# Two units' k and q transposed by DMA instead of by TensorE, in a retention and token-mixing kernel with a hand-written order

## The chip, the cores and the metric

The kernel runs on one core of one Trainium2 chip (trn2). The metric is the time of one launch on the device in microseconds; for the kernel before, the median of three runs is 164.52 us (164.24 to 164.79). Everything that is read from a profile comes from one further, profiled execution.

## The reference

Two stages, cut to what matters:

```python
# q, k, v: (4, 8, 768, 64) float32 (batch, heads, sequence, head width)
for t in range(S):                                    # per batch and head
    state = gamma * state + outer(k[t], v[t])
    y[t] = (1 / sqrt(D)) * q[t] @ state
x = heads side by side                                # (4, 768, 512)
theta = x @ w_theta
z_r, z_i = x * cos(theta), x * sin(theta)
u = x + w_tok_r @ z_r + w_tok_i @ z_i                 # mixes tokens: (768 x 768) @ (768 x 512), per batch
out = u + max(u @ w_ch, 0)
```

The recurrence is computed in chunks: inside a chunk of tokens as masked attention, from chunk to chunk through the state.

## The kernel before

The attention work is cut into 24 units. Unit n is one batch, 256 tokens (two chunks of 128) and half of the heads, so six units make a batch. The mixing work is cut into 24 tiles of 128 tokens. Units and tiles overlap: the mixing of one batch runs while the attention of the next one is under way.

Nothing schedules this but a table. `ORDER` is a long string of tokens; the kernel walks through it and calls one small function for each token, and each engine executes its instructions in just that order. A token is a step's name, its unit or tile, and sometimes the engine: `ck.13.a` is the cast of k of unit 13 on ScalarE (ACT), `.v` is VectorE (DVE), `.p` is GpSimd (POOL), `.s` the SyncE (SP) queue. Each engine and queue works its own steps off in order, and waits where data or a buffer is missing; tile pools with a fixed number of buffers decide when a buffer comes free.

The steps of unit n that matter here, with their lines:

- `Lk`, `Lq`, `Lv` (L156): loads of k, q and v of the unit, 256 KB each.
- `ck`, `cq`/`cqs`, `cv` (L136/L138, L304, L310): casts to bf16. k and q of the unit go into one tile kqb (five buffers), v into vb. `cqs` and `cv` multiply by a decay factor on the way.
- Transposing kqb into kqT, in one of three ways. `Tk` and `Tq` (L318) are eight 128x128 TensorE transposes into PSUM and `E` copies them out. `Tk6`, `Tq6` and `E6` (L337) do the same in 64x64 tiles, of which several fit into TensorE's array at once: 32 transposes and two copies. `Dk` (L367) is one DMA transpose, issued by the SP queue, with nothing on TensorE:

```python
    def Dk(n):
        kqT = work.tile([P, 2, 2, 2, P], BF, name="kqT", bufs=4)
        nc.sync.dma_start_transpose(
            out=kqT.rearrange("p w a j t -> p (w a j) t"),
            in_=st["kqb", n].rearrange("p w d -> p (w d)"))
        st["kqT", n] = kqT
```

- `A` (L380): scores from kqT. `m` (L389): mask, on VectorE. `ST` (L408): the unit's part of the state, from kqb and vb. `S0`, `S1` (L426, L430): the state's sums, on VectorE. `SB` (L136/L138): the state as bf16. `I` (L446) and `Y` (L458): output from the state, and from the scores, in the PSUM banks R0 and R1, each of which one unit holds at a time. `I` of a unit writes the banks that the unit before it used, so it waits for that one's `S0` and `S1`.
- `XA`, `XB` (L476, L136/L138): the output out of PSUM, as xT of a chunk. `Tx`, `Tx6`, `Dx` (L490, L337, L504): xT back into token order, by TensorE or by DMA.

And of the mixing:

- `Hh` (L511) is x @ w_theta of a chunk in a PSUM accumulator, `CN` (L518) the sine and cosine passes of ScalarE over it, `z` (L525) the product with x. `M` (L559) are the token-mixing matmuls of a tile, `u` (L566) adds x, `Tu`, `Tu6`, `Du` (L571, L337, L590) transpose u, `O` (L595) multiplies by w_ch, `f` (L601) finishes, `SO` (L606) stores. `Hh`, `M` and `O` share two accumulator banks.

`A`, `Y`, `ST` and all steps named with a 6 work on 64x64 tiles of TensorE's array; all others use the whole array.

Of the kernel before, what the change touches and what calls it, by code (L numbers as in the profile page):

```python
# [50 lines left out]
CN.10.1 Dx.11 Ex.10.v Lk.16.s Lv.17.s Hh.11 SO.2.s CN.10.0 m.12 S1.12 z.10.v cq.13.v M.6.1 M.6.2 M.6.0  # L51
M.6.3 CN.11.0 CN.11.1 M.7.3 SB.12.1.a Lk.17.a ck.13.a M.7.4 M.7.0 M.6.4 Dk.13 M.7.1 z.11.v SO.3.s A.14
Tu6.5 M.6.5 Eu6.5.0.a Eu6.5.1.a M.7.2 I.12 Lv.14.s u.6 cqs.15.v M.7.5 M.9.3 ck.17.a m.14 SO.4.a Lq.17.s
Lq.18.s Lk.21.s ck.16.a M.9.0 M.9.5 M.9.1 M.9.4 Lq.19.a M.9.2 Du.6 cv.13.v u.7 u.9 Y.12 cv.14.p ST.13
Tk6.15 Tq6.15 E6.15.0.v E6.15.1.v A.13 O.5 XB.12.1.a XB.12.0.a M.8.1 S0.13.a S1.13 M.8.4 M.8.3 SB.13.0.a
SB.13.1.p cq.16.p m.13 I.13 ck.18.a Y.13 ST.14 A.15 M.8.0 f.5 cq.17.v Lv.18.a M.8.5 M.8.2 XA.13.0
XA.13.1 S0.14.v SB.14.0.p Lv.16.s Hh.13 S1.14 u.8 M.10.1 cv.15.p cv.17.p SB.14.1.p M.10.0 M.10.4
cqs.18.v M.10.5 CN.13.0 CN.13.1 Hh.12 CN.12.1 I.14 m.15 Y.14 CN.12.0 ST.15 S0.15.v XB.14.1.a SB.15.0.a
M.10.3 cv.16.v Dk.16 Dk.17 Du.7 Dx.13 M.10.2 Dk.18 O.6 SB.15.1.p XB.14.0.v S1.15 I.15 Y.15 ST.16 Tx6.12
SO.5.a cv.18.p f.6 S0.16.v A.16 M.11.4 cq.19.p SB.16.1.p M.11.1 Lq.21.a Ex6.12.0.a Ex6.12.1.a z.12.p  # L60
SB.16.0.a Lk.19.s Lk.20.s XB.15.0.a u.10 z.13.p XB.15.1.a m.16 O.7 Du.10 I.16 Y.16 Tu6.8 ST.17 f.7
Eu6.8.0.v Eu6.8.1.a A.17 Hh.15 CN.15.1 CN.15.0 Dx.14 M.11.2 Tx.15 Lv.22.s SO.7.s M.11.0 M.11.5 S0.17.v
SB.17.0.p M.11.3 XA.16.1 m.17 XA.16.0 Ex.15.v Hh.14 SB.17.1.p z.15.p ck.21.p ck.19.p I.17 u.11 Tu6.11
A.18 Y.17 ST.18 Eu6.11.1.v S0.18.v XA.17.1 XA.17.0 O.10 SO.1.a S1.18 Lv.19.a CN.14.1 CN.14.0 Dx.16
Lq.20.a f.10 Lq.22.a SB.18.0.a Hh.17 Eu6.11.0.a SB.18.1.a I.18 Tk.19 Tq.19 CN.17.1 O.8 CN.17.0 m.18
E.19.a Hh.16 z.14.p Lv.20.s Du.9 f.8 O.11 Y.18 cv.19.p ck.20.a CN.16.1 ST.19 A.19 Tx6.17 CN.16.0 M.12.1
f.11 Ex6.17.0.v Ex6.17.1.v cq.20.p Lk.22.s Dk.20 M.12.0 S0.19.a M.13.3 M.13.2 XB.18.1.a SB.19.1.p
SB.19.0.v M.13.0 z.17.v cqs.21.v XB.18.0.v S1.19 z.16.v m.19 cv.20.v M.12.3 M.12.2 M.13.5 Lv.21.s M.13.1
M.12.4 M.12.5 I.19 M.13.4 Y.19 ST.20 u.12 A.20 Dk.21 XA.19.1 S0.20.v XA.19.0 ck.22.a cq.22.a SB.20.1.p
cv.22.p M.14.3 M.14.5 M.14.1 M.14.4 M.14.2 M.14.0 SB.20.0.p u.13 m.20 S1.20 Hh.19 I.20 Y.20 SO.10.s  # L70
Lq.23.s Lk.23.s cv.21.v u.14 A.21 ST.21 CN.19.0 CN.19.1 S0.21.v M.15.3 M.15.5 S1.21 m.21 XA.20.1 Hh.18
CN.18.1 CN.18.0 Dx.18 Dk.22 ck.23.a M.15.4 M.15.2 SB.21.0.p M.15.1 M.15.0 SB.21.1.v Lv.23.s Du.12 Dx.19
XA.20.0 O.9 f.9 I.21 Y.21 A.22 ST.22 M.16.1 cqs.23.p u.15 m.22 S0.22.v z.18.p z.19.p M.16.5 SB.22.0.p
M.16.4 O.12 M.16.0 SO.8.a M.16.2 M.16.3 SB.22.1.p XB.21.0.a XB.21.1.a SO.11.s Du.14 cv.23.p Dk.23 f.12
Du.13 Dx.20 Dx.21 Hh.21 u.16 I.22 A.23 Y.22 ST.23 CN.21.0 CN.21.1 Hh.20 CN.20.1 S0.23.v XA.22.1 XA.22.0
SB.23.0.a M.17.1 M.17.3 CN.20.0 M.17.0 SB.23.1.p I.23 M.17.2 m.23 Y.23 O.13 M.17.4 z.21.v M.17.5 Mh.0.1
Mh.0.3 XB.23.1.v f.13 Hh.23 u.17 XB.23.0.a SO.13.a CN.23.1 Du.16 Hh.22 z.20.v CN.22.1 Mh.0.2 M.19.3
Dx.23 CN.23.0 Dx.22 Mh.0.0 M.21.1 M.19.1 z.23.p CN.22.0 SO.6.a Du.17 M.18.1 O.16 M.21.2 M.19.2 M.19.0
M.18.3 f.16 SO.9.a M.18.5 z.22.p M.18.2 O.17 M.19.4 M.18.0 Mh.0.4 M.18.4 f.17 u.18 Du.15 SO.12.s O.15
M.19.5 f.15 u.19 SO.16.s M.22.2 M.22.1 O.14 Mh.0.5 uh.0 f.14 M.22.0 M.21.5 M.22.3 M.22.5 Du.19 M.21.4  # L80
SO.17.s M.22.4 Du.18 O.19 M.21.0 M.21.3 M.20.2 Mh.1.2 Mh.1.0 Mh.1.4 u.22 O.18 Mh.1.3 SO.15.a f.19 M.20.0
M.20.1 Tuh.0 u.21 Du.22 Du.21 f.18 M.20.3 Euh.0 M.20.4 Mh.1.1 M.20.5 u.20 O.22 Mh.1.5 uh.1 f.22 Tu.20
SO.14.a SO.19.s Eu.20.a O.21 SO.18.a Tuh.1 Euh.1 f.21 Oa.0 Oa.1 fa.0 fa.1 Oh.0 Oh.1 SO.21.a SO.22.s
SO.20.s fh.0 SOh.0 fh.1 SOh.1 Z.31
""".split()


# [618 lines left out]
```

## Time and profile before

| | |
|---|---|
| median of three runs | 164.52 us (164.24 to 164.79) |
| the profiled execution's own time | 164.61 us |
| its span, first to last instruction | 162.9 us |
| TensorE matmul busy | 154.2 us, 95% of the span |
| VectorE, ScalarE, GpSimd busy | 114.1, 79.6, 72.2 us |
| granted TensorE clock | 1.000 |
| DMA | 34.93 MB, mean 214 GB/s |

How to read it: busy time is what an engine spent in instructions. In a timeline each row is a start in us from the span's start, a duration, the engine, the line in the kernel, the operation, out<-in and a count; neighbouring rows of one kind are merged. Matmuls are pipelined, so the duration of a row overlaps the next one, and the time a step takes from TensorE is the distance from its start to the next start. A DMA's row on SP is the time that its issue took; its landing is told apart.

### The profile page before, as it was taken

The numbers are of one execution on the slowest core, as the hardware profiler recorded it, in microseconds if no ns is written. First come the engines' busy times: TensorE is split into PE (matmuls) and PEld (weight loads), VectorE is DVE, ScalarE is ACT, GpSimd is POOL, SyncE is SP. The second block draws the span as 40 slices with busy tenths as digits, with TensorE's granted clock in tenths as the row PEclk, the third lists the DMA queues.
The fourth block names the chain that finished last, engine by engine and source line by source line (L and its number), as shares of the span: only waits on it lengthen the run. The fifth ranks groups of instructions, "written<-read, shape, count | busy, mean of one in ns | idle before, by whom it ended". The sixth has DMA issues, their size and how long they took to land.

```text
span 162.9 us, 5079 instructions
## 1 busy us (share of the span) xinstructions
PE 154.2 (95%) x2108; PEld 86.0 (53%) x2108; DVE 114.1 (70%) x218; ACT 79.6 (49%) x148; POOL 72.2 (44%) x105
## 2 busy tenths in 40 slices
...
DMA packets 69062, 34.93 MB, mean 214 GB/s; under 512 B 26416, under 2 KB 66096, under 8 KB 69040
## 3 DMA queue, kind: packets, MB, share of 16 engines
...
q10 hardware_dynamic: 10320, 7.47, 16.0%
q0 software_dynamic: 2688, 3.41, 12.1%
q8 instruction: 16, 0.26, 0.7%
q14 instruction: 6, 0.05, 0.1%
...
## 4 chain that ended last, share of the span: by engine, by line
PE 79%; DMA 8%; ACT 5%; SPq 2%; POOL 2%; DVE 1%; issue 1%; POOLq 0%; ACTq 0%
PE y_ps L559 37%; PE o_ps L595 12%; PE th_ps L511 12%; DMA kqf<-in_k_dram 8%; PE r_ps L458 4%; ACT qx L232 3%; PE at_ps L380 3%; PE w_ps L533 2%; PE r_ps L446 2%; SPq L156 2%; PE kq_ps L318 2%; PE y_ps L620 2%; PE r_ps L408 1%; PE x_ps L490 1%; ACT kqb L136 1%
## 5 line engine op out<-in xcount | busy, mean ns | idle before, releaser
L559 PE MATMUL y_ps<-z,wtr 128*128 128x512 bf16 x138 | 52.4, 380 | 0.0
L559 PE MATMUL y_ps<-z,wti 128*128 128x512 bf16 x138 | 52.3, 379 | 0.0
L525 POOL TENSOR_TENSOR z<-cs,x_sb 128x1024 bf16<-128x1024 bf16 x12 | 25.5, 2138 | 17.2 <-ACT cs L518 10.7
L389 DVE TENSOR_TENSOR at<-at_ps,mask 128x1024 bf16<-128x1024 f32 x24 | 29.2, 1216 | 1.0 <-PE at_ps L380 1.0
L310 POOL TENSOR_TENSOR vb<-vf,vsc 128x512 bf16<-128x512 f32 x15 | 15.6, 1042 | 23.3 <-DMA vf<-in_v_dram 19.1
L566 DVE TENSOR_TENSOR u<-y_ps,x_sb 128x512 bf16<-128x512 f32 x23 | 15.8, 688 | 13.2 <-PE y_ps L559 13.1
L511 PE MATMUL th_ps<-wth,xT 128*128 128x512 bf16 x96 | 24.5, 379 | 0.4 <-ACT cs L518 0.4
L601 DVE SCALAR_TENSOR_TENSOR ot<-o_ps,u 128x512 f32<-128x512 f32 x22 | 15.2, 689 | 13.4 <-PE o_ps L595 13.2
L595 PE MATMUL o_ps<-wch,uT 128*128 128x512 bf16 x88 | 22.6, 379 | 0.0
L518 ACT ACTIVATE cs<-th_ps,halfpi 128x512 bf16<-128x512 f32 x24 | 16.3, 685 | 12.5 <-PE th_ps L511 6.9
L518 ACT ACTIVATE cs<-th_ps,zerob 128x512 bf16<-128x512 f32 x24 | 16.5, 686 | 10.6 <-PE th_ps L511 5.1
L559 PEld LDWEIGHTS <-wtr 128*128 128x128 bf16 x138 | 13.5, 98 | 13.2
L559 PEld LDWEIGHTS <-wti 128*128 128x128 bf16 x138 | 13.5, 98 | 12.6 <-issue 0.4
L138 POOL CAST sbd<-s 64x256 bf16<-64x256 f32 (+1 forms) x20 | 8.4, 420 | 21.2 <-DVE s L426 19.5
L136 ACT COPY kqT<-kq_ps 128x1024 bf16<-128x1024 bf16 (+1 forms) x11 | 10.7, 973 | 10.1 <-PE kq_ps L318 9.8
L511 PEld LDWEIGHTS <-xT 128*128 128x128 bf16 x96 | 8.8, 98 | 9.2 <-issue 0.8
L595 PEld LDWEIGHTS <-uT 128*128 128x128 bf16 x88 | 8.1, 98 | 8.3
L279 PE MATMUL zz<-zero 128*128 128x512 bf16 x30 | 10.0, 463 | 1.9 <-DVE zero L191 1.9
L136 ACT CAST kqb<-kqf 128x512 bf16<-128x512 f32 x16 | 9.6, 623 | 4.0 <-DMA kqf<-in_k_dram 4.0
L458 PE MATMUL r_ps<-at,vb 64*64 64x128 bf16 x384 | 10.0, 221 | 1.6 <-DVE at L389 1.6
L380 PE MATMUL at_ps<-kqT 64*64 64x128 bf16 x384 | 10.0, 219 | 0.4 <-DVE kqT L138 0.4
L318 PE MATMUL kq_ps<-ident,kqb 128*128 128x128 bf16 x104 | 9.3, 220 | 0.8 <-POOL kqb L304 0.6
...
## 6 DMA issues: line engine op xcount, KB each, us to landing
...
```

What stands on the lines that cost most here:

```text
L136: nc.scalar.copy(dst, src)
L310: engines[e].tensor_mul(in_blocks(vb), by_token(raw["vf", n]), _bcast_last(K["vsc"][:, i, :, h * HU:(h + 1) * HU], D))
L380: nc.tensor.matmul(at_ps[cols, g, j, a, :], kq_at(n, 0, a, j, c)[rows], kq_at(n, 1, slice(0, 2), j, c)[rows], start=(j == 0 and a == 0), s ...
L389: nc.vector.tensor_mul(at.rearrange("p g j a t -> p (g j) (a t)"), st["at_ps", n].rearrange("p g j a t -> p (g j) (a t)"), _bcast_mid(K["m ...
L458: nc.tensor.matmul(st["R", n + 1][c][g * D:(g + 1) * D, j * P:(j + 1) * P], st["vb", n][rows, lo:lo + D], st["at", n][rows, g, j, a, :], s ...
L511: nc.tensor.matmul(th_ps, st["xT", C][:, j, :], K["wth"][:, j, :], start=(j == 0), stop=(j == 3))
L518: nc.scalar.activation(st["cs", C][:, w, :], st["th_ps", C], AF.Sin, bias=K["zerob" if w else "halfpi"], scale=1.0)
L525: engines[e].tensor_mul(st["z", b][:, c], st["cs", C], _bcast_mid(x_of(C), 2))
L559: nc.tensor.matmul(st["y", t], K["wT"][r][:, s0, t0 * P:(t0 + 1) * P], st["z", b][:, s0, r, :], start=(done == 0 and r == 0), stop=(done = ...
L566: nc.vector.tensor_add(st["u", t], st["y", t], st["x", b][:, t0, :])
L595: nc.tensor.matmul(o_ps, st["uT", t][:, j, :], K["wch"][:, j, :], start=(j == 0), stop=(j == nD - 1))
L601: nc.vector.scalar_tensor_tensor(st["ot", t], st["o", t], 0.0, st["u", t], ALU.max, ALU.add)
```

## The change

Unit 15's `Tk6`, `Tq6` and two `E6`, and unit 19's `Tk`, `Tq` and `E`, are removed; `Dk.15` and `Dk.19` come in. The tokens `Lk.19.s` and `Lk.21.s` change places. Eight other tokens stand elsewhere than before: `Tu.0` (behind A.8), `O.1` (ahead of M.4.0), `ck.13.a` (earlier), `Dx.11` (behind Lk.16), `cqs.15.v` (right behind z.11), `S0.14.v` (ahead of XA.13.1), `ck.19.p` (from behind ck.21 up to behind SB.14.1), `A.18` (from ahead of Y.17 to behind Hh.17); and `I.18` and `Tx6.17` stand in another order to their neighbours than before. No function is changed. Two places of the table, cut:

```diff
-ST.13 Tk6.15 Tq6.15 E6.15.0.v E6.15.1.v A.13 O.5
+ST.13 A.13 O.5
...
-Tu6.11 A.18 Y.17 ST.18 ... O.10 ... Hh.17 Eu6.11.0.a SB.18.1.a I.18 Tk.19 Tq.19 CN.17.1 O.8 ... E.19.a Hh.16 ... O.11 Y.18 ... ST.19 A.19 Tx6.17
+Tu6.11 Y.17 ST.18 ... O.10 ... Hh.17 A.18 Eu6.11.0.a SB.18.1.a Tx6.17 CN.17.1 O.8 I.18 ... Hh.16 ... O.11 Y.18 ... ST.19 A.19
```

On the SP queue around `Dk.15`: the L606 row is the store of tile 3, the vf row the load of v of unit 14, and the rows behind are q of units 17 and 18 and k of unit 21 (before) or 19 (now).

```order
 L606 DMA out_dram<-ot 128x512
 L156 DMA vf<-in_v_dram 128x4x128
+L367 DMA_TRANSPOSE kqT<-kqb 128x8x128
 L156 DMA kqf<-in_q_dram 128x4x128 x2
 L156 DMA kqf<-in_k_dram 128x4x128
```

The transpose of unit 15 stands between a load and three loads that stood right behind one another.

On the SP queue around `Dk.19`: uT is the transpose of u of tile 10, x_sb that of chunk 14, and the vf row the load of v of unit 22.

```order
 L590 DMA_TRANSPOSE uT<-u 128x4x128
 L504 DMA_TRANSPOSE x_sb<-xT 128x4x128
+L367 DMA_TRANSPOSE kqT<-kqb 128x8x128
 L156 DMA vf<-in_v_dram 128x4x128
 L606 DMA out_dram<-ot 128x512
```

The transpose of unit 19 is a third transpose in a row, ahead of a load and a store.

On GpSimd around `ck.19`: the two vb rows in front are cv.15 and cv.17, the sbd rows are SB.14.1 and SB.15.1 (their numbers differ only because tiles are numbered anew), and behind them come cv.18 and cq.19.

```order
 L310 TENSOR_TENSOR vb<-vf,vsc 128x512 x2
-L138 CAST sbd_96<-s_1763 64x4x64
-L138 CAST sbd_98<-s_1990 64x4x64
+L138 CAST sbd_96<-s_1765 64x4x64
+L138 CAST kqb<-kqf 128x512
+L138 CAST sbd_98<-s_1955 64x4x64
 L310 TENSOR_TENSOR vb<-vf,vsc 128x512
 L138 CAST kqb<-kqf 128x512
```

The cast of k of unit 19 now stands between the two state copies, and no longer behind the cast of k of unit 21.

More of the change, by code (lines that the diff above doesn't have):

```diff
@@ L38 @@
 ck.8.a u.0 S0.7.v m.7 XA.6.1 SB.7.1.a M.1.5 M.1.3 XA.6.0 Tw.1.3 M.2.5 Pw.0.2 M.2.3 u.1 S1.7 Tk.8 M.2.1
-M.2.0 SB.7.0.v Ew.1.3.a Tu.0 I.7 cv.8.v E.8.a Lk.10.s cv.9.p Y.7 ST.8 A.8 cqs.9.v ck.9.v M.2.4 Du.1
+M.2.0 SB.7.0.v Ew.1.3.a I.7 cv.8.v E.8.a Lk.10.s cv.9.p Y.7 ST.8 A.8 Tu.0 cqs.9.v ck.9.v M.2.4 Du.1
 Eu.0.a XB.7.1.a XB.7.0.v S0.8.v SB.8.0.v M.2.2 Tx.6 Tq.9 Tk.9 Lv.10.a ck.10.p cv.10.p Lq.10.s S1.8 u.2
@@ L44 @@
 O.2 Lq.11.s Lk.11.s E.10.a Lk.15.s Ew.0.5.v Lk.14.s Y.9 ST.10 Tw6.1.5 Ew6.1.5.0.a Ew6.1.5.1.a A.10 z.7.p
-Lv.11.s XB.9.1.a XB.9.0.a f.2 M.4.0 O.1 M.4.1 cqs.14.p m.10 f.1 S0.10.v cq.11.a ck.12.v M.4.4 M.4.2 Tu.3
+Lv.11.s XB.9.1.a XB.9.0.a f.2 O.1 M.4.0 M.4.1 cqs.14.p m.10 f.1 S0.10.v cq.11.a ck.12.v M.4.4 M.4.2 Tu.3
 Eu.3.a Dx.9 SB.10.0.a cqs.12.p u.4 Hh.9 ck.11.v z.6.v ck.15.v M.5.0 M.5.4 Tk.11 Tq.11 E.11.a SB.10.1.p
@@ L50 @@
 E6.14.0.v E6.14.1.a Lv.15.s O.3 z.8.p XA.11.0 XA.11.1 Hh.10 A.12 S0.12.a f.3 z.9.v SB.12.0.v Tx.10
[L51 to L84, printed above, removed]
+ck.13.a CN.10.1 Ex.10.v Lk.16.s Dx.11 Lv.17.s Hh.11 SO.2.s CN.10.0 m.12 S1.12 z.10.v cq.13.v M.6.1 M.6.2
@@ new lines @@
+M.6.0 M.6.3 CN.11.0 CN.11.1 M.7.3 SB.12.1.a Lk.17.a M.7.4 M.7.0 M.6.4 Dk.13 M.7.1 z.11.v cqs.15.v SO.3.s
+A.14 Tu6.5 M.6.5 Eu6.5.0.a Eu6.5.1.a M.7.2 I.12 Lv.14.s Dk.15 u.6 M.7.5 M.9.3 ck.17.a m.14 SO.4.a
+Lq.17.s Lq.18.s Lk.19.s ck.16.a M.9.0 M.9.5 M.9.1 M.9.4 Lq.19.a M.9.2 Du.6 cv.13.v u.7 u.9 Y.12 cv.14.p
+ST.13 A.13 O.5 XB.12.1.a XB.12.0.a M.8.1 S0.13.a S1.13 M.8.4 M.8.3 SB.13.0.a SB.13.1.p cq.16.p m.13 I.13
+ck.18.a Y.13 ST.14 A.15 M.8.0 f.5 cq.17.v Lv.18.a M.8.5 M.8.2 XA.13.0 S0.14.v XA.13.1 SB.14.0.p Lv.16.s
@@ new lines @@
+Hh.13 S1.14 u.8 M.10.1 cv.15.p cv.17.p SB.14.1.p ck.19.p M.10.0 M.10.4 cqs.18.v M.10.5 CN.13.0 CN.13.1
+Hh.12 CN.12.1 I.14 m.15 Y.14 CN.12.0 ST.15 S0.15.v XB.14.1.a SB.15.0.a M.10.3 cv.16.v Dk.16 Dk.17 Du.7
+Dx.13 M.10.2 Dk.18 O.6 SB.15.1.p XB.14.0.v S1.15 I.15 Y.15 ST.16 Tx6.12 SO.5.a cv.18.p f.6 S0.16.v A.16
+M.11.4 cq.19.p SB.16.1.p M.11.1 Lq.21.a Ex6.12.0.a Ex6.12.1.a z.12.p SB.16.0.a Lk.21.s Lk.20.s XB.15.0.a
+u.10 z.13.p XB.15.1.a m.16 O.7 Du.10 I.16 Y.16 Tu6.8 ST.17 f.7 Eu6.8.0.v Eu6.8.1.a A.17 Hh.15 CN.15.1
@@ new lines @@
+CN.15.0 Dx.14 Dk.19 M.11.2 Tx.15 Lv.22.s SO.7.s M.11.0 M.11.5 S0.17.v SB.17.0.p M.11.3 XA.16.1 m.17
+XA.16.0 Ex.15.v Hh.14 SB.17.1.p z.15.p ck.21.p I.17 u.11 Tu6.11 Y.17 ST.18 Eu6.11.1.v S0.18.v XA.17.1
+XA.17.0 O.10 SO.1.a S1.18 Lv.19.a CN.14.1 CN.14.0 Dx.16 Lq.20.a f.10 Lq.22.a SB.18.0.a Hh.17 A.18
+Eu6.11.0.a SB.18.1.a Tx6.17 CN.17.1 O.8 I.18 CN.17.0 m.18 Hh.16 z.14.p Lv.20.s Du.9 f.8 O.11 Y.18
+cv.19.p ck.20.a CN.16.1 ST.19 A.19 CN.16.0 M.12.1 f.11 Ex6.17.0.v Ex6.17.1.v cq.20.p Lk.22.s Dk.20
@@ new lines @@
+M.12.0 S0.19.a M.13.3 M.13.2 XB.18.1.a SB.19.1.p SB.19.0.v M.13.0 z.17.v cqs.21.v XB.18.0.v S1.19 z.16.v
+m.19 cv.20.v M.12.3 M.12.2 M.13.5 Lv.21.s M.13.1 M.12.4 M.12.5 I.19 M.13.4 Y.19 ST.20 u.12 A.20 Dk.21
+XA.19.1 S0.20.v XA.19.0 ck.22.a cq.22.a SB.20.1.p cv.22.p M.14.3 M.14.5 M.14.1 M.14.4 M.14.2 M.14.0
+SB.20.0.p u.13 m.20 S1.20 Hh.19 I.20 Y.20 SO.10.s Lq.23.s Lk.23.s cv.21.v u.14 A.21 ST.21 CN.19.0
+CN.19.1 S0.21.v M.15.3 M.15.5 S1.21 m.21 XA.20.1 Hh.18 CN.18.1 CN.18.0 Dx.18 Dk.22 ck.23.a M.15.4 M.15.2
```

13 lines of the change are left out of this document (added).

## Prediction, before the changed kernel was run

> **What bounds the kernel now.** I read the page, then the windows, then TensorE's timeline around units 15 and 19, then the engines and the queue that feed it there.
>
> ```profile
> span 162.9 us, 5079 instructions
> PE 79%; DMA 8%; ACT 5%; SPq 2%; POOL 2%; DVE 1%; issue 1%; POOLq 0%; ACTq 0%
> core 0: us, PE busy (x) PEld busy (x) DVE busy (x) ACT busy (x) POOL busy (x), PEclk, DMA share, GB/s
> 60.00:100.00 40.00, 40.00 (x649) 21.69 (x651) 32.07 (x60) 19.67 (x43) 19.14 (x21) 1.00 1.23 244
> 100.00:130.00 30.00, 30.00 (x438) 15.84 (x430) 22.88 (x45) 13.29 (x27) 15.50 (x18) 1.00 0.97 197
> ```
>
> The chain that ended last is TensorE for 79% of the span, and in both windows TensorE is busy in every microsecond, at full clock. Nothing but TensorE's own row of instructions sets the end there: what leaves that row leaves the time, unless something new makes TensorE wait. The windows also show the DMA engines loaded (share 1.23, then 0.97), and the change moves work to them.
>
> **Unit 15: what leaves TensorE.** The rows give starts; a step costs the distance to the next start, since ends overlap.
>
> ```profile
> 80.64 0.29 PE L408 MATMUL r_ps<-vb,kqb 64*64 64x64 bf16 x16
> 80.76 0.43 PE L337 MATMUL kq_ps<-ident,kqb 64*64 64x64 bf16 x32
> 81.02 0.43 PE L380 MATMUL at_ps<-kqT 64*64 64x128 bf16 x16
> ...
> 84.12 0.40 PE L380 MATMUL at_ps<-kqT 64*64 64x128 bf16 x16
> ```
>
> The 32 small transposes Tk6.15 and Tq6.15 start at 80.76 and A.13 behind them at 81.02: 0.26 us go. Steps of 64x64 tiles stand on both sides, so nothing else changes in that place. The two copies E6.15 leave VectorE, which is not the bound: no gain. The row at 84.12 is A.15, which now waits for the transfer instead.
>
> **Unit 19: what leaves TensorE, and what comes in.** TensorE from A.18 to the end of Tx6.17, before:
>
> ```profile
> 99.99 0.40 PE L380 MATMUL at_ps<-kqT 64*64 64x128 bf16 x16
> 100.22 0.39 PE L458 MATMUL r_ps<-at,vb 64*64 64x128 bf16 x16
> 100.44 0.29 PE L408 MATMUL r_ps<-vb,kqb 64*64 64x64 bf16 x16
> 100.67 1.04 PE L595 MATMUL o_ps<-wch,uT 128*128 128x512 bf16 x4
> 101.54 1.03 PE L511 MATMUL th_ps<-wth,xT 128*128 128x512 bf16 x4
> 102.40 0.28 PE L446 MATMUL r_ps<-kqT,sbd 128*128 128x128 bf16 x2
> 102.52 0.61 PE L318 MATMUL kq_ps<-ident,kqb 128*128 128x128 bf16 x8
> 102.96 1.03 PE L595 MATMUL o_ps<-wch,uT 128*128 128x512 bf16 x4
> 103.98 1.02 PE L511 MATMUL th_ps<-wth,xT 128*128 128x512 bf16 x4
> 104.84 1.03 PE L595 MATMUL o_ps<-wch,uT 128*128 128x512 bf16 x4
> 105.80 0.42 PE L458 MATMUL r_ps<-at,vb 64*64 64x128 bf16 x16
> ...
> 106.17 0.40 PE L380 MATMUL at_ps<-kqT 64*64 64x128 bf16 x16
> 106.40 0.29 PE L337 MATMUL x_ps<-ident,xT 64*64 64x64 bf16 x16
> 106.62 0.39 PE L559 MATMUL y_ps<-z,wtr 128*128 128x512 bf16 x1
> ```
>
> ```profile
> 103.25 0.68 ACT L518 ACTIVATE cs<-th_ps,halfpi 128x512 bf16<-128x512 f32 x1
> ```
>
> The eight transposes of unit 19 take 102.96 - 102.52 = 0.44. But a change between full steps and 64x64 steps has a price: four full 512-wide matmuls take 0.87 before another full step (100.67 to 101.54) and 0.96 before a small one (104.84 to 105.80), so 0.10 going in; sixteen L408 steps take 0.23 before a full step (100.44) against 0.12 before a small one (80.64), so 0.10 coming out. Before, A.18 stood in one group of small steps and Tx6.17 in another. The change puts both into a third group between Hh.17 and O.8, which costs 0.20 more.
>
> It isn't 0.44 - 0.20, though, because one stretch has a floor. Hh.16 (103.98) takes the accumulator that ScalarE's second sine pass of Hh.17 frees at 103.25 + 0.68 = 103.93. From Hh.17's start to Hh.16's start are 2.44 us; TensorE has 0.86 + 0.12 + 0.44 + 0.86 = 2.28 of work in it and waits 0.16. After the change the work is 0.86 + 0.10 + 0.23 (A.18) + 0.22 (Tx6.17, on the way out) + 0.86 + 0.12 = 2.39, still under 2.44. So the stretch keeps its length: the 0.44 is not gained there. The gain lies at its two ends. A.18 leaves the group before it: 0.23. Tx6.17 leaves the group behind it, which ran from 105.80 to 106.62, 0.82, and now takes 0.60 (to 106.40) and 0.10 for the way out: 0.12. Together 0.35 (0.24 if the floor were not there, so I take the rows).
>
> **What the moves risk.** The cast ck.19 on POOL now stands ahead of SB.15.1, and takes the buffer of k and q of unit 15, so it starts when ST.15 (89.86) is over. There VectorE runs cv.16, which reads two SBUF operands.
>
> ```profile
> 82.59 0.61 POOL L138 CAST kqb<-kqf 128x512 bf16<-128x512 f32 x1
> 85.75 2.04 POOL L310 TENSOR_TENSOR vb<-vf,vsc 128x512 bf16<-128x512 f32 x2
> 86.57 1.77 DVE L304 TENSOR_TENSOR kqb<-kqf,qsc 128x512 bf16<-128x512 f32 x1
> 89.86 0.29 PE L408 MATMUL r_ps<-vb,kqb 64*64 64x64 bf16 x16
> 90.41 0.68 DVE L310 TENSOR_TENSOR vb<-vf,vsc 128x512 bf16<-128x512 f32 x1
> ...
> 91.35 0.28 DVE L430 TENSOR_TENSOR s<-r_ps,s 128x128 f32<-128x128 f32 x1
> 91.82 0.39 PE L446 MATMUL r_ps<-kqT,sbd 128*128 128x128 bf16 x4
> ```
>
> Such a VectorE step is held while POOL works: cqs.18 (86.57) took 1.77, not 0.68, and ended 0.55 after POOL did (85.75 + 2.04 = 87.79). On the clock of before, ck.19 runs from 90.15 to some 90.8, so cv.16 ends near 91.35 and not 91.09, and S1.15 (ends at 91.63) near 91.9. The second half of I.15 (91.82, half of its 0.22 later, 91.93) needs S1.15. Between 0 and 0.3 us; I take 0.05, as the slack all but covers it.
>
> Dk.15 goes onto SP behind Lv.14, and shifts the loads and transposes behind it.
>
> ```profile
> L367 SPq DMA_TRANSPOSE kqT<-kqb x9: 1232/1242/3513, 60.5 to 122.3; - x9
> DMA to landing us min/median/max: 3.3/5.0/6.3
> 73.84 0.69 DVE L525 TENSOR_TENSOR z<-cs,x_sb 128x1024 bf16<-128x1024 bf16 x1
> 76.20 0.44 SPq L156 DMA_DIRECT2D vf<-in_v_dram  x1
> 76.69 2.49 SPq L156 DMA_DIRECT2D kqf<-in_q_dram  x2
> DMA to landing us min/median/max: 6.0/6.0/6.0
> 83.88 0.42 DVE L138 CAST kqb<-kqf 128x512 bf16<-128x512 f32 x1
> 93.91 1.20 SPq L590 DMA_TRANSPOSE uT<-u  x1
> DMA to landing us min/median/max: 4.9/4.9/4.9
> ```
>
> The first two rows are the nine kqT transposes: issue 1.24 on SP, and landing 5.0 after it, 6.3 at worst. cqs.15 now follows z.11 (74.53) at once, so Dk.15 is issued by 76.7 and lands between 80.0 and 83.0. A.15 wants it at 84.12 - 0.26 = 83.86: covered by 0.9 in the worst row. Dk.19 goes out behind Dx.14, near 97 to 98, lands by 104.3 at worst, and A.19 (106.17 - 0.6) wants it at 105.6: covered. The load of q of unit 17 (76.69, landed 6.0 later at 82.7) shifts by up to 1.24, to 83.9; its cast stood at 83.88, 83.6 on the new clock: 0 to 0.3 lost, I take 0. The exchanged loads of k cost nothing: k of unit 19 comes 13 us earlier and k of unit 21 is cast only at 100.8. ScalarE loses a 1.01 us copy and stays off the bound. Tu.0 and O.1, ahead of these windows, trade places with steps that TensorE does anyway and leave its groups as they are: 0. ck.13 and S0.14 only come earlier on their engines, and where ck.13 stood ScalarE is not the bound: 0. Dx.11 lets a load of k go ahead of it; if that held z.11 by a load's whole issue (1.2, half of the 76.69 row), z.11 would end at 75.7 and cqs.15 at 76.4, and Dk.15 would still go at 76.7: 0, and without that cover at most what A.15's 0.9 doesn't take up.
>
> A page speaks against the change. The Trainium skill, "VectorE: DVE Perf Modes", section "The three transpose paths", gives 1309 ns for a 128x128 block by DMA against 390 ns on TensorE. By it, as an estimate, the eight blocks of a unit would take 10.5 us by DMA. The trace has 5.0 (6.3 at most) and 0.44 on TensorE, and the measurement decides.
>
> **The sum.** The profiled execution took 164.61 (span 162.9). 164.61 - 0.26 - 0.35 + 0.05 = 164.05; the median of the three runs shown, 164.52, lies 0.09 lower: 163.96, so 164.0. A measurement of this kernel can tell about 0.3%, 0.49 us, from no change; the forecast lies just past it.
>
> **Rivals.**
> Small waits eat it: ck.19's hold on cv.16 costs its 0.3, and the late q of unit 17 its 0.3. For it: both slacks are under 0.1 us. Against: each takes the worst end. 163.96 + 0.25 + 0.3 = 164.5 if both, 164.2 with one: no change. Chance 0.30.
> The SP queue becomes late (slower): from 83 to 98 SP issues almost without a pause, and one kqT issue took 3.51, where the queue was full. Everything behind Dk.15 shifts, uT of step 10 among it: issued at 93.91, landed 4.9 later at 98.81, wanted by O.10 at 100.67 - 0.26 - 0.23 = 100.18. So a shift of 1.37 is free; Dk.15's own 1.24 fits just under it. If the queue fills a second time, the shift is 3.51 and O.10 waits 2.1: 166.1. It turns slower than before past a shift of about 2.4. Chance 0.12.
> The transposes are late: if Dk.15 takes over 7.2 us, A.15 waits the rest; at 8.3 us (6.3 and the 2.0 more that two loads ahead might add) 1.1 is lost: 165.1. The page's price would make it 10.5 - 7.2 = 3.3 us, 167.3, but no kqT row comes near it. Chance 0.05.
> More than forecast: the 2.44 stretch also shortens by its 0.16 wait, and the cast costs nothing: 163.7. Chance 0.08.
> The forecast, 163.8 to 164.1: 0.45.
>
> **How the numbers follow.** The two cases at or below the forecast hold 0.53, of which 0.06 lies within 0.3% of before: faster 0.47. That 0.06 and the small waits make same 0.36. The two late cases make slower 0.17. The range runs from 163.6, below the case with more, to 165.1, the lesser of the late cases; what it leaves out is most of the SP case.
>
> **What would show it.** Right: no L337 rows near 80.8, A.13 0.26 earlier; no L318 rows at 102; L380 and L337 together between L511 and L595; Hh.17 to Hh.16 still 2.44 apart; TensorE ahead by 0.26 at 90 and 0.6 at 107, and so to the end. Wrong: idle time of PE before L380 near 84 (Dk.15 late), before L446 near 91.6 (POOL's hold), or before L595 near 100.2 with uT as releaser.

## The result: 171.5 us, 4.2% slower, and the profile after

| | before | after |
|---|---|---|
| median | 164.62 us (164.24 to 164.88, 6 runs) | 171.52 us (170.86 to 172.19, 6 runs) |
| ratio to before | | 1.0423 [1.0392, 1.0453] |
| the profiled execution, its span | 164.61, 162.9 us | 172.19, 170.5 us |

The forecast was 164.0 and its range ended at 165.1. In all comparisons below, ratios and their intervals leave out runs that were disturbed by a lower clock or stood far above the kernel's other runs, while medians are of all runs.

The page of after first: the span, TensorE's busy tenths in 40 slices of 4.3 us, and the shares of the chain that ended last.

```profile
span 170.5 us, 4975 instructions
PE   5896799999989999999879999289999999999993
PE 70%; DMA 15%; DVE 6%; POOL 3%; issue 2%; SPq 1%; ACT 1%; DVEq 0%; POOLq 0%; ACTq 0%
```

Before, TensorE was 79% of that chain and DMA 8%. Now DMA has 15%, and TensorE has a hole (the 2 in its row, around 108 us). The windows that were full before, and the 20 us behind the hole by themselves:

```profile
60.00:100.00 40.00, 37.77 (x580) 20.14 (x586) 30.11 (x55) 18.84 (x42) 16.36 (x19) 1.00 1.10 213
100.00:130.00 30.00, 25.67 (x357) 13.19 (x362) 19.67 (x39) 10.37 (x21) 15.07 (x15) 0.94 0.99 202
110.00:130.00 20.00, 18.51 (x246) 9.61 (x251) 14.18 (x28) 4.61 (x9) 6.43 (x7) 0.91 0.86 172
```

TensorE idles 2.23 + 4.33 us in the first two, where it was busy throughout at full clock, and behind the hole its clock is 0.91. That is most of the 7.6 us by which the span grew. Compared by the starts of the same steps (L458), TensorE is 2.7 us behind the kernel before at 103 us, 6.5 at 112, and 7.7 from 120 on; the last 1.2 are the clock's. Of the view of waits, these are TensorE's waits that are new or have grown (total, times, longest):

```profile
PE o_ps L595 <- DVE ot L601: 3.4, 1, 3.4
PE th_ps L511 <- DVE xT L476: 0.6, 1, 0.6
PE w_ps L533 <- DVE s L426: 0.5, 1, 0.5
PE r_ps L446 <- DVE ot L601: 0.5, 1, 0.5
PE at_ps L380 <- DMA kqT<-kqb: 0.3, 1, 0.3
```

The largest is one wait of `O.11` for an accumulator that VectorE's `f.8` frees. The chain of waits shows where it began, 32 us earlier (start, duration, what):

```profile
78.51 8.21 DMA kqf<-in_q_dram
86.74 0.43 DVE kqb L138
...
92.22 1.27 SPq L590
93.61 5.78 DMA x_sb<-xT
...
103.62 6.65 DMA out_dram<-ot
110.37 0.70 DVE ot L601
111.11 0.38 PE o_ps L595
```

The load of q of unit 17 stands behind `Dk.15` on SyncE. It was issued at 78.51 and landed at 86.72; before, it was issued at 76.69 and landed at 82.7. SyncE's timeline after:

```profile
76.79 1.65 SPq L367 DMA_TRANSPOSE kqT<-kqb  x1
78.51 2.77 SPq L156 DMA_DIRECT2D kqf<-in_q_dram  x2
...
82.50 3.03 SPq L590 DMA_TRANSPOSE uT<-u  x1
...
86.79 5.39 SPq L367 DMA_TRANSPOSE kqT<-kqb  x2
...
101.61 1.29 SPq L367 DMA_TRANSPOSE kqT<-kqb  x1
102.95 0.58 SPq L156 DMA_DIRECT2D vf<-in_v_dram  x1
103.62 0.51 SPq L606 DMA_DIRECT2D out_dram<-ot  x1
```

and before:

```profile
79.97 1.41 SPq L590 DMA_TRANSPOSE uT<-u  x1
...
83.23 5.12 SPq L367 DMA_TRANSPOSE kqT<-kqb  x2
...
97.41 0.46 SPq L606 DMA_DIRECT2D out_dram<-ot  x1
```

`Dk.16` starts 0.07 us after the late load has landed, 3.6 us later than before, and everything behind it on SyncE is late with it. Most of this is issue time: SyncE was done with the row ahead of `Dk.16` (the load of v of unit 16) at 82.01 before, and then waited till 83.23 for a cast on POOL; after, it is done with that row only at 86.16. `Dk.15` itself took 1.65 of these 4.15 us, and the transposed u of tile 6 (the L590 row) 3.03 instead of 1.41. The late load added the last 0.6. From `Dk.16` on SyncE issues almost without a pause, so the 3.6 us reach the store of tile 7 (the L606 row), and `Dk.19` (1.3) and longer issues add 2.6: it goes out at 103.62 instead of 97.41. `f.8` takes the output buffer that this store reads, so VectorE waits for it to land (idle time in brackets):

```profile
86.74 0.43 DVE L138 CAST kqb<-kqf 128x512 bf16<-128x512 f32 x1 [2.56 <-DMA kqf<-in_q_dram]
110.37 0.69 DVE L601 SCALAR_TENSOR_TENSOR ot<-o_ps,u 128x512 f32<-128x512 f32 x1 [3.46 <-DMA out_dram<-ot]
```

And the transfers from 76 to 88 us, in 40 slices of 0.3 us, GB/s, after and then before:

```profile
GB/s 401 360 276 230 276 336 207 345 275 341 269 289 131 89 37 40 24 15 20 18 216 149 189 203 147 135 300 191 288 287 290 294 287 292 292 283 311 276 294 299
```

```profile
GB/s 382 310 285 271 388 406 319 248 307 364 326 364 335 350 340 355 343 341 338 301 306 288 274 287 133 60 45 35 21 332 224 288 289 317 266 302 193 12 18 10
```

For 2.1 us, from 79.9 to 82.0, while `Dk.15` is in flight, under 90 GB/s move. Before, it was 300 to 355 there. A transfer that was issued ahead of `Dk.15` is late as well: the load of v of unit 14 (76.19, and 76.20 before) landed at 82.61 instead of 80.99. Its cast on POOL and the state copy SB.13.1 behind it are late, and `I.13` waited 0.5 us for them (the L446 row above, where the view names VectorE).

**Eight semaphores.** That `Dk.16` should wait for a load of q that it doesn't read has its reason in the built program. The loads, transposes and stores of SyncE's and ScalarE's queues share eight completion semaphores, given out in turn in the program's order, and each waits until the transfer that had its semaphore before has landed. On SyncE after, with what each row waits for as the program names it (DMAHW0 to DMAHW7 are the eight, and a transfer that waits for one of them raises the same one): `Dk.15`, the load of q of unit 17, then the load of v of unit 16 and `Dk.16`:

```
L367 DMA_TRANSPOSE kqT<-kqb 128x8x128 [waits DMAHW7_49,DVE_49,PE_49]
L156 DMA kqf<-in_q_dram 128x4x128 [waits DMAHW0_49]
...
L156 DMA vf<-in_v_dram 128x4x128 [waits DMAHW7_49]
L367 DMA_TRANSPOSE kqT<-kqb 128x8x128 [waits PE_49,DMAHW0_49,Activation_49,Pool_49]
```

The load of v waits for `Dk.15`, and `Dk.16` for the load of q. In the traces of before, of after and of twelve kernels of this study there are 1778 transfers with such a predecessor. Apart from 13 with records missing, none starts earlier than 0.015 us after the predecessor's landing, and 157 start within 0.1 us of it. So a late transfer doesn't only delay its readers: it can hold the eighth transfer behind it, and with that one its whole queue. For `Dk.16` that was 0.6 us here; in unit 19's kernel below two such waits are 1.8 and 2.5 us.

### The profile page after: what moved, and what is told of

It reads as the page before. It is cut to its first block, busy times and chain, and to the rows that moved or that the text cites. A ratio compares the mean times of both kernels' runs of the same rounds, so it can differ in the third digit from the quotient of the medians.

```text
span 170.5 us, 4975 instructions
## 1 busy us (share of the span) xinstructions
PE 154.3 (91%) x2040; PEld 85.5 (50%) x2068; DVE 114.6 (67%) x216; ACT 78.6 (46%) x147; POOL 73.5 (43%) x105
## 4 chain that ended last, share of the span: by engine, by line
PE 70%; DMA 15%; DVE 6%; POOL 3%; issue 2%; SPq 1%; ACT 1%; DVEq 0%; POOLq 0%; ACTq 0%
PE y_ps L559 30%; PE th_ps L511 9%; PE o_ps L595 9%; DMA kqf<-in_q_dram 8%; DMA out_dram<-ot 4%; PE r_ps L458 4%; DMA x_sb<-xT 3%; PE at_ps L380 3%; PE kq_ps L318 3%; PE r_ps L446 2%; PE w_ps L533 2%; DVE at L389 2%; PE y_ps L620 2%; PE r_ps L408 2%; POOL z L525 1%
## 5 line engine op out<-in xcount | busy, mean ns | idle before, releaser
L559 PE MATMUL y_ps<-z,wtr 128*128 128x512 bf16 x133 | 51.0, 383 | 0.7 <-issue 0.2
L559 PE MATMUL y_ps<-z,wti 128*128 128x512 bf16 x130 | 49.5, 381 | 0.6 <-issue 0.5
L138 POOL CAST sbd<-s 64x256 bf16<-64x256 f32 (+1 forms) x20 | 9.5, 474 | 26.3 <-DVE s L426 20.8
L136 ACT COPY kqT<-kq_ps 128x1024 bf16<-128x1024 bf16 (+1 forms) x10 | 9.7, 969 | 9.7 <-PE kq_ps L318 9.3
L458 PE MATMUL r_ps<-at,vb 64*64 64x128 bf16 x384 | 10.2, 225 | 1.6 <-DVE at L389 1.6
L279 PE MATMUL zz<-zero 128*128 128x512 bf16 x28 | 9.5, 466 | 2.0 <-DVE zero L191 1.9
L380 PE MATMUL at_ps<-kqT 64*64 64x128 bf16 x384 | 10.2, 223 | 0.7 <-DVE kqT L138 0.4
L476 DVE TENSOR_TENSOR xT<-r_ps,qx 128x256 bf16<-128x256 f32 x22 | 8.8, 417 | 2.2 <-DMA x_sb<-xT 0.9
```

Source lines behind the costliest of these rows:

```text
L136: nc.scalar.copy(dst, src)
L380: nc.tensor.matmul(at_ps[cols, g, j, a, :], kq_at(n, 0, a, j, c)[rows], kq_at(n, 1, slice(0, 2), j, c)[rows], start=(j == 0 and a == 0), s ...
L458: nc.tensor.matmul(st["R", n + 1][c][g * D:(g + 1) * D, j * P:(j + 1) * P], st["vb", n][rows, lo:lo + D], st["at", n][rows, g, j, a, :], s ...
L559: nc.tensor.matmul(st["y", t], K["wT"][r][:, s0, t0 * P:(t0 + 1) * P], st["z", b][:, s0, r, :], start=(done == 0 and r == 0), stop=(done = ...
```

## The experiments

| kernel | median, us | ratio to before |
|---|---|---|
| moves only, no transpose by DMA | 166.12 | 1.0106 [1.0071, 1.0142] |
| the two early moves only | 165.94 | 1.0081 [1.0052, 1.0111] |
| unit 15 only | 168.16 | 1.0194 [1.0123, 1.0264] |
| unit 15 without the early moves | 166.59 | 1.0112 [1.0058, 1.0166] |
| unit 15, a load in place of Dk.15 | 165.77 | 1.0085 [1.0054, 1.0116] |
| unit 15, an extra transpose there | 169.21 (166.24 to 171.45) | unclear |
| unit 15 without early moves, k of unit 21 late | 165.68 | 1.0061 [1.0031, 1.0091] |
| unit 15, Dk.15 in SyncE's idle time | 164.89 | 1.0029 [1.0008, 1.0050] |
| unit 19 only | 168.10 | 1.0111 [1.0023, 1.0200] |
| all, SO.7 on ScalarE | 167.91 | 1.0160 [1.0070, 1.0250] |
| unit 19, SO.7 on ScalarE | 164.75 | 1.0026 [0.9998, 1.0055] |
| the same, v of unit 22 late | 164.15 | 0.9983 [0.9959, 1.0007] |
| both units placed | **163.86** | **0.9963 [0.9935, 0.9992]** |
| early moves, code shifted | 168.14 | 1.0248 [1.0184, 1.0311] |
| code shifted | 167.56 (165.40 to 169.06) | 1.0101 [1.0036, 1.0167] |

The kernel before had medians of 164.23 to 164.50 beside them.

### The change in parts

Unit 15 alone (its transposes and the moves that belong to it; unit 19 as before):

```diff
-ST.13 Tk6.15 Tq6.15 E6.15.0.v E6.15.1.v A.13
+ST.13 A.13
-Lv.14.s u.6 cqs.15.v
+Lv.14.s Dk.15 u.6
```

> Only unit 15's part of the change (Dk.15 and the moves that belong to it: Tu.0, O.1, ck.13, Dx.11, cqs.15, S0.14); unit 19 stays on TensorE. Theory 'queue' (a transpose put into the full SP queue costs the DMA engines far more than its issue, and everything behind it lands about 4 us late): 167 to 169 us, with waits of TensorE before A.15 and before M.10, and q of unit 17 landing near 86. Theory 'store' (the damage is the store SO.7 that Dk.19 pushes back, so that f.8 has no buffer): 164.3 us, since Dk.19 is not there.

It costs 1.9% by itself, as the theory of the queue had it, but not by the waits that I expected, ahead of A.15 and M.10. Two of its waits on TensorE, and the cast of q of unit 17 on VectorE:

```profile
PE o_ps L595 <- DMA uT<-u: 1.8, 2, 1.3
PE w_ps L533 <- DVE xT L476: 1.5, 1, 1.5
```

```profile
86.39 0.43 DVE L138 CAST kqb<-kqf 128x512 bf16<-128x512 f32 x1 [0.96 <-DMA kqf<-in_q_dram]
```

Most of the first is one wait, at 97.3, of `O.7` for the transposed u of tile 7, which landed 5.1 us after its issue, and 2.5 before. The second lies near 50 us, long before unit 15's transpose: it belongs to the moves.

Unit 19 alone (the exchanged loads, ck.19, A.18, Tx6.17, Dk.19):

```diff
-Dx.14 M.11.2 Tx.15 Lv.22.s SO.7.s
+Dx.14 Dk.19 M.11.2 Tx.15 Lv.22.s SO.7.s
```

> Only unit 19's part (Dk.19, the exchanged loads of k, ck.19, A.18, I.18, Tx6.17); unit 15 stays on TensorE. Theory 'queue': by 97 us the backlog is small, so Dk.19 costs little: 164.0 to 165.0 us, SO.7 lands by 104. Theory 'store': 167.5 to 169 us, with 3 us of TensorE idle before O.11, as in the changed kernel.

```profile
PE o_ps L595 <- DVE ot L601: 3.0, 1, 3.0
```

Of TensorE's waits beyond those of before this is the large one: `O.11` on `f.8`, with SO.7 issued at 99.51 and landed at 106.27. The theory of the store named it; the 1.1%, 1.8 us, are less than the 3 us and more that it expected. The whole change with that one store issued by ScalarE:

```diff
-SO.7.s
+SO.7.a
```

> The changed kernel with one letter changed: the store SO.7 goes out on ScalarE's queue, not behind Dk.19 on SP's. Theory 'queue': the 3.4 us before O.11 go, and the clock's dip behind them (1 us), but the waits between 82 and 104 stay (some 3.5 us): 167 to 168 us. Theory 'store': 164 to 165 us.

The wait is gone, and 1.6% slower stays of 4.2%. TensorE now waits for the transposed u of tile 7 (in a profile at a clock of 0.978):

```profile
PE o_ps L595 <- DMA uT<-u: 2.9, 1, 2.9
```

So the store made 1.7 to 3.5 points of the 4.2, by the interval of the second ratio, and unit 15 and the moves the rest. The moves alone, with both units' transposes on TensorE, and with `I.18` and `Tx6.17` in the order of before:

```diff
-Dk.15   -Dk.19
+Tk6.15 Tq6.15 E6.15.0.v E6.15.1.v   +Tk.19 Tq.19 E.19.a
```

> The moves without the DMA transposes: units 15 and 19 transposed on TensorE as before, but Tu.0, O.1, ck.13, Dx.11, cqs.15, S0.14, ck.19, A.18 and the exchanged loads of k where the changed kernel has them (I.18 and Tx6.17 as before, since Tx6.17 ahead would block the PSUM buffers). Theories 'queue' and 'store': 164.4 to 165.0 us, no change but for the extra group of small steps. Theory 'moves' (POOL's hold at ck.19, or the regrouped steps, cost the time): 167 us or more.

They cost 1.1% without any transfer added; 166.12 lies between the two times expected:

```profile
PE w_ps L533 <- DVE xT L476: 1.2, 1, 1.2
```

### The two early moves: a wait for code

```diff
-Ew.1.3.a Tu.0 I.7 ... A.8 cqs.9.v      M.4.0 O.1 M.4.1
+Ew.1.3.a I.7 ... A.8 Tu.0 cqs.9.v      O.1 M.4.0 M.4.1
```

> The kernel before with only the two earliest moves, Tu.0 behind A.8 and O.1 ahead of M.4.0; all transposes as before, no load exchanged. Theory 'fetch': the 1.2 us that TensorE lost before a w_ps step (L533) at 49.7 in the kernel with the moves alone comes from these two, because TensorE then reaches the end of a block of its instructions while the transfer queues are full: there the instruction queue's one 16 KB packet took 3.2% of 16 engines in 6 us, 3.1 us, against 1.0%, 0.96 us, before. It expects this long packet and a wait of 1.0 to 1.3 us before an L533 step near 50, and 165.2 to 165.6. Rival 'elsewhere': the moves cost nothing by themselves and the 1% came from the casts moved later on (ck.13, cqs.15, ck.19): 164.1 to 164.5 and no such wait.

165.94 is just above what the theory of code (fetch) expected, and the early moves hold most of what the moves cost. The DMA view for 45 to 51 us lists the queue that brings TensorE's instructions, one packet of 16 KB, with its share of 16 engines in 6 us. Moves only; then early moves only; then before:

```profile
q8 instruction: 1, 0.02, 3.2%
```

```profile
q8 instruction: 1, 0.02, 2.0%
```

```profile
q8 instruction: 1, 0.02, 1.0%
```

3.2% of 16 x 6 us are 3.1 us, and before it was 0.96. In the seven kernels that have the early moves and TensorE's code otherwise in place (after, unit 15 only, moves only, the early moves, all with SO.7 moved, a load for Dk.15, and an extra transpose) the packet ended between 48.55 and 49.84, and TensorE's next step started 1.3 to 1.7 us behind that end each time; in eight without the early moves it ended by 47.6 and nothing waited. The view of waits names VectorE's xT (L476) as the releaser, which was long done. To tell code from data, 84 instructions more at the start, which move the places where packets are asked for, with the early moves and without:

```diff
-Z.8  Z.28  Z.39
+Z.8.16  Z.28.16  Z.39.16
```

> The kernel with only the two early moves (165.94), and 84 more TensorE instructions in its first 7 us: three warm-up products of zeros (Z.28, Z.39, Z.8) in 16 pieces each instead of 2, of the same columns in all. Theory 'fetch': TensorE's code comes in packets of 16 KB, and the 1.1 us before Tw.0.3 (L533, 49.4) are a wait for the packet that began at 47.6 and took 1.9 us. 84 instructions are about a third of a packet, so this packet is asked for 1.5 to 2 us earlier, its end falls before TensorE needs it, the wait at 49.4 goes, and the time is 164.3 to 165.0. Rival 'data': the wait is for the step's operands, which the early moves made late; it stays at 0.9 to 1.3 us in the same place, and the time is 165.6 to 166.3.

> The kernel before with the same 84 additional TensorE instructions and no move: the control. If they cost nothing at the start, 164.2 to 164.9. Theory 'fetch' allows a wait for code in a new place, seen as a long packet of the instruction queue, of up to 1 us; rival 'data' expects none.

The wait at 49.4 went, as a wait for code would and one for data would not. But 168.14 is far above what was expected, since a new wait came up at 97, in the middle of a step of 64x64 tiles whose first part had run (early moves, code shifted):

```profile
96.48 0.28 PE L380 MATMUL at_ps<-kqT 64*64 64x128 bf16 x4
98.77 0.36 PE L380 MATMUL at_ps<-kqT 64*64 64x128 bf16 x10 [2.00 <-issue]
```

There a packet began at 96.09 and took 1.12, and TensorE went on 1.56 us behind its end. The control has the same wait (1.1 us, 1.40 behind the end of a packet that began at 96.67), and is slower than before too. These distances are those of the wait near 50. Not all of 168.14 is this wait: behind it the granted clock was 0.50 for 3.4 us. So a wait for code fits every one of these kernels, and the times expected of both shifted kernels failed: I had reckoned with the one place and not with the others that the shift moves. Why the packet near 47 took up to 3.1 us isn't settled.

### Unit 15: the transpose, not its bytes

A plain load of 256 KB in Dk.15's place, TensorE transposing as before:

```diff
-Lv.14.s Dk.15 u.6
+Lv.14.s Ld u.6
```

> The kernel with only unit 15 changed, but at Dk.15's place in SyncE's row stands a plain load of the same 256 KB (q of unit 15 once more, into a tile that nothing reads), and TensorE transposes k and q of unit 15 as before. It tells whether the price is that of any transfer in this place or of the transpose. Theory 'transpose': a load takes the engines about 0.9 us (256 KB at the 290 GB/s of the fullest slices), so the load of q of unit 17, 86.4 behind Dk.15, lands by 84.5 and u.8 and the uT of step 7 are not late; with the 1.1 us of the early moves the time is 165.2 to 165.9. Rival 'any transfer': the load of q of unit 17 lands near 86 as well, and the time is 167.5 to 168.5, as with Dk.15.

165.77, no more than the early moves cost without it. The same with an idle transpose of the same bytes:

```diff
-Lv.14.s Ld u.6
+Lv.14.s Dd u.6
```

> As the kernel with an extra load in Dk.15's place (165.77), but with an extra DMA transpose of k and q of unit 15 there, into a tile that nothing reads; TensorE transposes them too, as before, so A.15 waits for no transfer. The same 256 KB, in the same row of the queue. Theory 'transpose': what unit 15 cost beyond the early moves (168.16 against 165.8) is the price of a transpose among loads, so 167.6 to 168.6 here, with the load of q of unit 17 landing near 86. Rival 'chain': it came through what waits for Dk.15's result (A.15) and its later row of TensorE steps, and an idle transpose costs what the idle load cost: 165.5 to 166.2.

Its four runs lie between 166.24 and 171.45, so its price in time can't be told, but the profiled one (168.9, clock 1.00) shows what happens to the traffic. GB/s in slices of 0.2 us from 78 to 86, with the idle transpose and then with the load:

```profile
GB/s 415 313 312 333 302 302 332 137 67 26 20 19 28 64 248 187 143 157 259 138 94 281 183 223 124 238 174 264 287 294 294 287 289 284 300 292 292 277 302 289
```

```profile
GB/s 133 95 212 246 341 348 384 397 305 328 330 341 287 264 266 335 307 310 338 351 343 343 305 305 294 302 294 294 292 270 279 277 174 90 47 38 40 20 18 24
```

The hole near 80 comes with the transpose and not with the load; it stands near there in the other kernels with `Dk.15` among the loads, too. With the load the next hole begins at 84.6, where the transposed u of tile 6 and `Dk.16` are in flight. After the hole at 80 VectorE waited 1.21 us for q of unit 17, and TensorE 1.9 us for u of tile 7.

Dk.15 in its place, but without the early moves:

```diff
-Ew.1.3.a I.7 ... A.8 Tu.0 cqs.9.v      O.1 M.4.0 M.4.1
+Ew.1.3.a Tu.0 I.7 ... A.8 cqs.9.v      M.4.0 O.1 M.4.1
```

> The kernel with only unit 15 changed (168.16), without its two early moves: Tu.0 and O.1 stand as before, everything else of unit 15's change stays, Dk.15 among the loads too. Theory 'ring': the early moves' 1.3 us go and the price of Dk.15's place, near 2.3 us, stays: 166.4 to 167.2, with Dk.16 again started within 0.1 us of the landing of Lq.17. Rival 'traffic of the moment': the place costs only because the early moves had shifted TensorE against the transfers, so that without them Lq.17 lands by 84.5 and the time is 164.6 to 165.7, as in the kernel with k of unit 21 late (165.68).

166.59: 1.1% for the place, and with the 0.8% of the early moves the 1.9% of unit 15 alone. `Dk.16` started 0.08 us after Lq.17 landed, at 84.17 here. The theory of the ring had the time and this start; but Lq.17 landed by 84.5, as the rival had it. Where the time went:

```profile
PE o_ps L595 <- DMA uT<-u: 1.7, 2, 1.4
```

Most of it is again the wait of `O.7`, at 95.2, for the transposed u of tile 7: issued at 89.98, landed at 95.11. With the plain load in `Dk.15`'s place the same transfer went out at 89.75 and landed at 92.23, and nothing waited, though `Dk.16` had gone out later there, at 84.66. So neither the late q nor its semaphore makes the price of this place by itself. The slower transpose of u does, and why it took 5.1 us instead of 2.5 isn't shown. From this kernel, one load moved:

```diff
-Lq.17.s Lq.18.s Lk.21.s
+Lq.17.s Lq.18.s
-Dk.18 O.6
+Dk.18 Lk.21.s O.6
```

> The kernel with only unit 15 changed (168.16), without the two early moves (Tu.0 and O.1 as before) and with the load of k of unit 21 moved from behind Lq.18 to behind Dk.18, so that Dk.16 shares its semaphore with Dk.15 (landed 84.50 there) and no longer with Lq.17 (landed 86.37, and Dk.16 started 0.08 us later). The early moves cost 1.3 us alone, so without them 166.8 to 167.0 stays if nothing else helps. Theory 'ring': Dk.16 goes out near 84.7 instead of 86.45, and what follows on SyncE (Dk.17, uT of 7, x of 13) with it, so most of the rest goes: 164.8 to 165.8. Rival 'silence': the cost is the transfer engines' own standstill while Dk.15 runs, whatever waits for whom: 166.5 to 167.2.

165.68 is a time that the ring theory expected, with `Dk.16` at 82.70, 0.08 us behind the landing of `Dk.15`. But the intervals of the two kernels overlap, and the edit takes a load out of the crowd as well, so that SyncE comes to `Dk.16` at 81.60 and not at 83.40: how much is the semaphore and how much the load stays open. The hole is there too (10 to 20 GB/s from 78.8 to 79.9), so it doesn't cost 1.1% each time. Last, Dk.15 where SyncE had nothing to issue:

```diff
-Ex.8.v Y.11 ... Lv.15.s O.3
+Ex.8.v cqs.15.v Y.11 ... Lv.15.s Dk.15 O.3
```

> The kernel before with k and q of unit 15 transposed by DMA, and of the moves only cqs.15, which goes to VectorE ahead of f.4, so that Dk.15 is issued near 68, where SyncE had nothing to issue from 65.3 to 69.7. Theory 'place': what unit 15 cost (3.6 us) came from Dk.15 standing among seven loads at 76.8; here it lands by 74 (5 to 6 us) and delays little behind it, so the predicted 0.26 us is gained, less up to 0.4 for VectorE's longer row: 163.9 to 164.6. Rival 'transfer': the transfer engines are loaded everywhere from 60 to 100 (share 1.23), so a transpose costs the following loads its 2 to 3 us wherever it stands, and steps behind them wait 1 to 2 us: 165.3 to 166.5.

It landed 5.6 us after its issue at 68.04, and of the 2% of unit 15 alone 0.3% are left. The traffic falls to 6 to 26 GB/s there from 71.1 to 72.6, but so it does before (9 to 28, 71.7 to 72.9). 164.89 lies between the two times expected.

### Unit 19: the store, then the semaphore

```diff
-SO.7.s
+SO.7.a
```

> The kernel with only unit 19 changed, and the store SO.7 issued by ScalarE instead of SyncE, so that it stands behind neither Dk.19 nor the load Lv.22. Theory 'store': the 3.0 us that TensorE waited before O.11 for f.8, which waits for the buffer that SO.7 holds, go; what is left is the gain that was predicted for unit 19, 0.35 us, so 163.8 to 164.0, 0.2 to 0.4% below before. Rival 'queue': the extra transpose Dk.19 delays the rows behind it by itself (uT of steps 9 and 10, x of 16), so another wait of 1 to 2 us takes the store's place: 165 to 166.

The 3.0 us went, and `A.20` waited for `Dk.20` instead, as the rival had said that some wait would; 164.75 lies between the two. TensorE's and SyncE's waits from 96 to 113:

```profile
PE at_ps L380 <- DMA kqT<-kqb: 1.6, 1, 1.6
```

```profile
SPq L590 <- DMA vf<-in_v_dram: 2.5, 1, 2.5
SPq L156 <- DMA kqT<-kqb: 1.8, 1, 1.8
```

A transpose of u that waits for a load of v, and a load of v that waits for a transpose of k and q: no data links them, only the semaphore. With the load of v of unit 22 later:

```diff
-Lv.22.s SO.7.a ... Dk.20 M.12.0
+SO.7.a ... Dk.20 Lv.22.s M.12.0
```

> The kernel with only unit 19 changed and SO.7 on ScalarE's queue (164.75), with one load more moved: v of unit 22 (Lv.22), which is wanted ten microseconds later, goes behind Dk.20. Theory 'ring': the two transfer queues share eight completion semaphores, given out in turn, and a transfer isn't issued before the one eight ahead of it has landed; there Lv.20 started 0.02 us after Dk.19 landed (104.04) and Du.9 0.07 us after Lv.22 landed (106.94), and with them Dk.20 went out 4.2 us later than before (109.90 against 105.74), for which A.20 waited 1.6 us. Without Lv.22 in between, Lv.20 waits for Dx.14 and Du.9 for Dk.19, Dk.20 goes out near 106, A.20's wait goes, and the time is 163.0 to 163.5, 0.6 to 0.9% below before. Rival 'engines': Dk.20 is late because the transfer engines are full from 97 to 107; one 256 KB load later changes that by 0.9 us at most, so A.20 still waits 0.7 us or more, and the time is 163.9 to 164.7.

Both semaphore waits and `A.20`'s are gone and `Dk.20` goes out at 106.75 instead of 109.90. 164.15 is below before, though the interval reaches 1.0007, and less was gained than the ring theory expected: the time is in the rival's range. Both units together:

```diff
-Ex.8.v Y.11 ... Lv.15.s O.3 ... Dx.14 M.11.2 Tx.15 Lv.22.s SO.7.s ... Dk.20 M.12.0
+Ex.8.v cqs.15.v Y.11 ... Lv.15.s Dk.15 O.3 ... Dx.14 Dk.19 M.11.2 Tx.15 SO.7.a ... Dk.20 Lv.22.s M.12.0
```

> Both units by DMA, each placed where its transfer finds room: unit 15 as in the kernel with Dk.15 in SyncE's idle time (164.89), unit 19 with SO.7 on ScalarE's queue and Lv.22 behind Dk.20; Tu.0 and O.1 stay where they were. Theory 'place': the two add up, and what the change was meant to take from TensorE (0.26 and 0.35 us) shows at last: 162.9 to 163.7. Rival 'sum of transfers': two more transposes in a queue that is loaded from 60 to 110 find a new wait behind them, in whichever place: 164.2 to 165.5.

163.86 against 164.50: 0.9963 [0.9935, 0.9992], the fastest kernel here, between the two times expected.

## Why the prediction was wrong

**What left TensorE was right.** After, no L337 rows stand near 81 and L380 follows L408 at once (80.90, then 81.02). From Hh.17 to Hh.16 are still 2.44 us (104.25 to 106.69). A.18 and Tx6.17 stand together in their third group:

```profile
105.21 0.42 PE L380 MATMUL at_ps<-kqT 64*64 64x128 bf16 x16
105.46 0.29 PE L337 MATMUL x_ps<-ident,xT 64*64 64x64 bf16 x16
105.68 1.04 PE L595 MATMUL o_ps<-wch,uT 128*128 128x512 bf16 x4
```

The kernel with both units placed gains 0.64 us, where the terms make 0.61; that they agree so well is partly luck. Its TensorE is 0.3 us ahead of before at 83 us and 0.65 from 112 on, so unit 19's 0.35 shows. Unit 15's 0.26 shows behind `A.13`, but is lost again by small waits such as that of `I.13` for SB.13.1, and a lead of 0.4 us stood there at 57 us already, ahead of the first edited step. The interval, 0.1 to 1.1 us, bears out the sign and no more than the rough size.

**The step that failed: "Dk.15 ... shifts the loads and transposes behind it" by its issue, 1.24.** The load of q of unit 17 was to land at 83.9 at worst and landed at 86.72, 4.0 later than before: 1.8 from the issue, and 2.2 because the transfer itself took 8.2 instead of 6.0. I took the queue's cost as one issue on SyncE and left out what a transpose does to transfers beside it. The bandwidth rows had it in view: before, too, they fall to 21 GB/s at 84.4, while the transposed u of tile 6 and `Dk.16` are in flight. Not every transpose does it: before, `Dk.13` is in flight from 74.26 to 78.09, and no slice before 78 is under 271 GB/s. Nor did the issue stay at 1.24: at `Dk.16` SyncE was 4.15 us late, since `Dk.15` took 1.65 and issues behind it grew.

**"6.3 at worst" failed.** `Dk.15` took 8.4. The nine rows of before were no bound; none stood among as many loads, which may be why. A.15 then waited 0.27 for it, less than the rival's 1.1, because A.15 was late itself.

```profile
DMA to landing us min/median/max: 3.1/4.0/8.4
```

The price of 1309 ns a block (the Trainium skill, "VectorE: DVE Perf Modes", "The three transpose paths"), 10.5 us for eight as an estimate, is nearer to this transfer than to the 5.6 of the one in idle time. It fits neither.

**Of what stands behind Dk.15 and Dk.19 I followed uT of step 10 and no store.** The SP rival (0.12) had the right mechanism and the wrong victim: not `O.10` on its uT at a shift of 1.37, but `O.11`, through `f.8`, the output buffer and SO.7, at a shift of 6.2. `Dk.16`'s shift, 3.6, is close to the rival's 3.51, but what it said of a single full queue doesn't cover the rest. Its 166.1 was too little by 5.4.

**A wait that the prediction didn't have** is the eighth transfer's: the late load of q held `Dk.16`, and with it SyncE. Here it is the smaller part, 0.6 us beside the 4.15 of issues.

**"Tu.0 and O.1 ... 0" failed by 1.3 us** in the kernel with these two alone; in after the wait is 0.5. That TensorE's groups stay as they are was true, and didn't settle it: the wait was, by all that the runs show, for code.

**The term for ck.19, 0.05, was 0.** The cast ran at 91.03, as soon as POOL's step ahead of it was done (90.22 + 0.74), and cv.16 took its plain 0.68. It didn't wait for unit 15's buffer, as ST.15 ran only at 92.03. My order of buffers was wrong.

```profile
90.22 0.74 POOL L138 CAST sbd<-s 64x256 bf16<-64x256 f32 x1
91.03 0.61 POOL L138 CAST kqb<-kqf 128x512 bf16<-128x512 f32 x1
92.59 0.68 DVE L310 TENSOR_TENSOR vb<-vf,vsc 128x512 bf16<-128x512 f32 x1
```
